# Padding the tiles of split x by 32 bytes, in a Fourier-mixing and mixture-of-experts kernel

## The chip, the core and the metric

The kernel runs on one core of a Trainium2 chip. The metric is device microseconds of one execution; less is better. Before the change the median of 3 timed runs is 762.34 us (760.38 to 762.79).

## What is computed

A layer norm of x (2048 tokens, 512 features) goes through a two-dimensional Fourier transform of which the real part is kept, and x is added. A second layer norm goes through a router that picks one of 8 experts for each token, and that expert's two matrices; the result is added again. In the reference:

```python
a = jnp.einsum("bsd,ed->bse", x, dft_hid_re)
b = jnp.einsum("bsd,ed->bse", x, dft_hid_im)
y = jnp.einsum("ts,bse->bte", dft_seq_re, a) - jnp.einsum("ts,bse->bte", dft_seq_im, b)
...
h = x + _A_ref(_layernorm(x, axis=-1), A_dft_seq_re, A_dft_seq_im, A_dft_hid_re, A_dft_hid_im)
h2 = h + _B_ref(_layernorm(h, axis=-1), B_w_gate, B_w1, B_w2)
```

With one expert per token the softmax over the picked logit is 1, so an expert's output is silu(x w1) w2 for its own tokens.

## The kernel before

Float32 accuracy is reached by splitting each operand into a high part in float32r and the rest, also float32r. `split` (L92) makes both, ScalarE the high part and VectorE the rest, and `mm3` (L129) turns one product into three matmuls: rest of the stationary operand by high part of the moving one (L131), high by rest (L132), high by high (L133). In the trace these three lines carry nearly all of TensorE's work, in every stage; the tiles' names tell the stage.

**The sequence stage**, from about 8 to 447 us of the span. x is normalised and split once, by `start` (L227) and `slot` (L197), into 16 tiles `xh0` to `xh15` and 16 tiles `xl0` to `xl15` of 128 partitions by 512 columns (2,048 bytes per partition), which stay in the pool `keep` (L165, L166). The sequence matrices come in blocks of 128 by 1024 into `raw`, and are split into `whi` and `wlo` (four buffers of each, 4,096 bytes per partition, pool `ring`). There are 8 chunks c of 256 output rows, and 8 blocks g to a chunk. For each block the loop of L482 to L486 goes over the four column groups k of 128, and inside over the two halves u of the block; tile s = 2g + u of x is the stationary operand (128 columns of it), half u of `whi` or `wlo` the moving one with 512 columns, and the four accumulators `p` take turns by k. So three matmuls use tile 2g, then three use tile 2g + 1, then the next k. That makes 8 x 8 x 8 x 3 = 1,536 matmuls of 512 columns. Behind a chunk the four accumulators are split into `ph` and `pl`, and `second` (L399) makes the transform over the features for two tiles of tokens, 24 matmuls each with `ph` and `pl` as stationary operands and `dh` and `dl` as moving ones (L408); it stands between blocks of the next chunk. `finish` (L297) does the residual, the norm and the router's logits.

**Routing.** `place` (L387) makes one-hot tiles of the tokens' ranks. It allocates them under the names `xh0` to `xh15` again, in the places of x tiles that are no longer read. L515 reads 14 of them as moving operands.

**The expert stage**, from about 464 us. Eight experts by 11 blocks of weights, again split into `whi` and `wlo`. `first` (L630) has the weights as stationary operand and the tokens `th`, `tl` as moving ones (256 to 304 columns); `then` (L645) does the second matrix, with the hidden activations `hh`, `hl`. Where the capacity is 256, `then` has `hh` and `hl` as stationary operands and the second half of `whi` and `wlo` as moving ones, 512 columns (L656). The tiles of this stage lie in the pool `moe`, which begins where `keep` began.

PE, VectorE, ScalarE and SP run in the order in which the kernel is written (a manual schedule); no planner and no table moves anything.

**Where the tiles lie.** In the built program the addresses are in bytes within a partition. The four `whi` buffers begin at 52,320, 56,416, 60,512 and 64,608, the four `wlo` at 68,704 to 80,992 in the same steps. `xh0` begins at 85,088, and the 32 tiles of split x follow each other in steps of 2,048. So every tile of split x and every half of `whi` and `wlo` has the same address modulo 2,048, which is 1,120, and modulo 512 it is 96; the 128 columns of a stationary operand begin at a multiple of 512 bytes in the tile. `dh`, `dl`, `ph` and `pl` have 96 modulo 512 too. In the expert stage the three `hh` buffers begin at 107,392, 108,608 and 109,824, the three `hl` at 111,040, 112,256 and 113,472: 288, 480, 160, 352, 32 and 224 bytes, modulo 512, from the halves of `whi` and `wlo`.

Of the kernel before, what the change touches and what calls it, by code (L numbers as in the profile page):

```python
# [9 lines left out]
F32R = mybir.dt.float32r  # L10
# [9 lines left out]
P = 128  # L20
S, D, F, E = 2048, 512, 1376, 8
EPS = 1e-5
NS = S // P
# [12 lines left out]

HOT = (5, 3, 2, 2, 0)
FAR = 2 * S

AHEAD = 7  # L40

# [2 lines left out]
def fnet_moe(ctx: ExitStack, tc: tile.TileContext, x, wseq, dhid, wgate, wcol, wexp, out):  # L44
# [23 lines left out]
    tok = const.tile([P, NS], F32, name="tok")  # L68
    nc.gpsimd.iota(tok, pattern=[[P, NS]], base=-FAR, channel_multiplier=1, allow_small_or_imprecise_dtypes=True)

# [87 lines left out]
    with ExitStack() as pa:  # L158
        keep = pa.enter_context(tc.tile_pool(name="keep", bufs=1))
# [2 lines left out]
        py = pa.enter_context(tc.tile_pool(name="py", bufs=1, space=PSUM))  # L162
        pr = pa.enter_context(tc.tile_pool(name="pr", bufs=1, space=PSUM))

        xh = [keep.tile([P, D], F32R, name=f"xh{s}") for s in range(NS)]  # L165
        xl = [keep.tile([P, D], F32R, name=f"xl{s}") for s in range(NS)]  # L166
        xts = {}

        def load_x(s):
# [215 lines left out]
        places = {}  # L385

        def place(t):  # L387

            q = places[t] = keep.tile([P, D], F32R, name=f"xh{t}")
            for c in ((slice(EARLY, NQ * P), slice(0, EARLY)) if t == NS - 1 else (slice(0, NQ * P),)):  # L390
                nc.vector.tensor_scalar(q[:, c], lanes[:, c], rank[:, t:t + 1], None, op0=ALU.is_equal)

# [6 lines left out]
        def second(t, ph, pl, xt, late=False, between=None):  # L399
            ps = pp.tile([P, D], F32, name="p") if between is not None else py.tile([P, D], F32, name="y")  # L400
            j = t % (TC // P)
            n = 0
            for k in range(KD):
                if k == KD - 1 and between is not None:
                    next(between)
                for im in range(2):
                    col = slice(im * TC + j * P, im * TC + (j + 1) * P)
                    mm3(ps, (ph[k][:, col], pl[k][:, col]), (dh[:, k, im, :], dl[:, k, im, :]), n == 0, n == 2 * KD - 1)  # L408
                    n += 1
            return finish(t, ps, xt, late, t >= NS - 4)  # L410
# [25 lines left out]
        for c in range(NC):  # L436
            ps = [pp.tile([P, 2 * TC], F32, name="p") for _ in range(KD)]
            for g in range(NS // 2):
# [25 lines left out]
                if c == NC - 1:  # L464
                    if g == 1:
                        cards(0, NS - 4)
                        ranks(0, NS - 4, group)
                    for t in range(max(0, 2 * g - 4), 2 * g - 2):
                        place(t)
                advance()  # L470
                if c == NC - 1 and g == NS // 2 - 1:
                    cards(NS - 4, NS - 2)
                    ranks(NS - 4, NS - 2, group)
                    for t in (NS - 4, NS - 3):
                        place(t)
                    nc.vector.tensor_copy(early, seen[:, NL, 0:1])
                    nc.vector.memset(seen[:, NL, 0:1], float(EARLY // P))
# [4 lines left out]
                for k, u in turns:  # L482
                    s = 2 * g + u
# [24 lines left out]
        f = second(NS - 2, ph, pl, last[0], True)  # L508
# [15 lines left out]
        nc.scalar.copy(whole, tb[:, :NQ * 2 * E])  # L524
        nc.gpsimd.tensor_scalar(src0, table[:, :, 0, 0], float(FAR), float(NL * P - 1), op0=ALU.add, op1=ALU.min)

# [3 lines left out]
        def fetch0(to, of, i):  # L530
            n, src, of = (P, src0[:, i:i + 1], of[:NL * P, :]) if i < EARLY // P else (LATE, src1, of)
            nc.gpsimd.indirect_dma_start(
                out=to[:n, i, :], out_offset=None, in_=of, in_offset=bass.IndirectOffsetOnAxis(ap=src[:n, :], axis=0))
# [8 lines left out]
        rk = before_them(NL, NL + 1)  # L542
        ranks(NL, NL + 1, rk)
        place(NL)
        next(g)
        warm = work.tile([P, 1], F32, name="warm")
# [9 lines left out]
        for _ in range(HOT[1]):  # L556
# [6 lines left out]
        nc.vector.tensor_scalar(  # L563
            src1, tb[:, late * 2 * E:late * 2 * E + 1], float(FAR), float(S - 1), op0=ALU.add, op1=ALU.min)
        fetch0(xg0, frows, late)
# [15 lines left out]
    with ExitStack() as pb:  # L581
# [9 lines left out]
        def home(tids):  # L591
            ids = work.tile([P, NQ], I32, name="ids", bufs=3)
            nc.vector.tensor_scalar(ids, tids, float(FAR), None, op0=ALU.add)
            return ids

        def whence(tids):

            src = work.tile([P, NQ], I32, name="src", bufs=3)
            nc.vector.tensor_scalar(src, tids, float(FAR), float(S - 1), op0=ALU.add, op1=ALU.min)
            return src, home(tids)  # L600
# [198 lines left out]
        for n in range(len(steps) + LAG):  # L799
# [26 lines left out]
            if n >= LAG:  # L826
# [12 lines left out]
                if j == 0 and done:  # L839
                    q, yT = done.pop()  # L840
# [3 lines left out]
        q, yT = done.pop()  # L844
# [6 lines left out]
        with tc.For_i(0, blocks, 1):  # L851
# [11 lines left out]
            spot = work.tile([P, NS], F32, name="spot")  # L863
            nc.vector.tensor_scalar(spot, whom, best, float(FAR), op0=ALU.not_equal, op1=ALU.mult)
            nc.vector.tensor_add(spot, spot, rank)
# [4 lines left out]
            for i, (lo, n) in enumerate(both):  # L870
                ps = pt.tile([P, D], F32, name="tp")
                for t in range(NS):
                    q = work.tile([P, P], F32R, name="q")
# [76 lines left out]
```

## Time and profile before

| | before |
|---|---|
| median of 3 timed runs | 762.34 us |
| profiled execution | 754.38 us |
| its span | 752.5 us |
| PE busy | 734.9 us (98%) |
| PE weight loads busy | 636.2 us |
| VectorE busy | 469.1 us |
| ScalarE busy | 260.8 us |
| POOL busy | 185.6 us |
| L131, L132, L133 with `xl`, `xh` | 512 matmuls each, mean 392, 390, 390 ns |
| chunks of data moved | 114.4 MB, mean 152 GB/s |

The profiled execution took 754.38 us, 752.5 of them between the first and the last instruction. Matmuls are pipelined: one is in the array for some 390 ns, while the next starts long before that, so the sum of the means is far more than the busy time, and the distance between starts is what a matmul costs. The granted clock is 1.00 where PE runs at 2.4 GHz, and 0.5 at 1.2 GHz.

### The profile page before, as it was taken

To read this page: it belongs to the slowest core of one execution; us is meant where nothing else is said; L and a number is where in the kernel's file an instruction comes from. 1 tells how busy PE (TensorE), PEld (TensorE's weight loads), DVE (VectorE), ACT (ScalarE), POOL (GpSimd) and SP (SyncE) were. 2 spreads that over 40 slices of the span, in tenths; PEclk is the share of its full clock that TensorE was granted. 3 is DMA by queue.
4 is the path that set the end of the run, shared out by engine and by line. 5 is a ranking of instruction groups with operands and counts; after the bars stand their busy time and mean duration, and the time that the engine had idled before them with its cause. 6 is when DMAs were issued, how large, how long until landed. Compare 5 with 4: busy or idle time off the path is not lost. (4 is left out here: it accounts for less than half of the span.)

```text
span 752.5 us, 10584 instructions
## 1 busy us (share of the span) xinstructions
PE 734.9 (98%) x3998; PEld 636.2 (85%) x3999; DVE 469.1 (62%) x1042; ACT 260.8 (35%) x391; POOL 185.6 (25%) x194
## 2 busy tenths in 40 slices
PE   8999999999999999999999999999999999999993
PEld 5888888888888888888888877999999999999992
DVE  8975754745745736636644566667677787777771
ACT  6872121131121121121121123444545455555550
POOL 3210000000000000000000003648484746647311
PEclk9999999999999999999999998999999999999997
DMA  8646324233323232332322423755666666667610
GB/s 293 238 166 249 118 85 138 90 110 109 125 99 112 99 125 84 122 103 85 126 98 84 141 84 95 241 209 180 219 203 200 213 224 226 230 225 236 210 57 29
DMA packets 34647, 114.40 MB, mean 152 GB/s; under 512 B 4751, under 2 KB 4751, under 8 KB 34464
## 3 DMA queue, kind: packets, MB, share of 16 engines
q0 software_dynamic: 17600, 60.70, 23.7%
q1 hardware_dynamic: 16992, 52.98, 20.2%
q8 instruction: 33, 0.54, 0.3%
q14 instruction: 22, 0.18, 0.1%
HBM read 101.07 MB, written 12.78 MB: 151 GB/s over the span
## 5 line engine op out<-in xcount | busy, mean ns | idle before, releaser
L131 PE MATMUL p<-whi,xl 128*128 128x512 f32 x512 | 200.7, 392 | 0.9 <-DVE xl L265 0.8
L132 PE MATMUL p<-wlo,xh 128*128 128x512 f32 x512 | 199.9, 390 | 0.0
L133 PE MATMUL p<-whi,xh 128*128 128x512 f32 x512 | 199.8, 390 | 0.0
L94 DVE TENSOR_TENSOR wlo<-far,whi 128x1024 fp32r<-128x1024 f32 x77 | 94.3, 1224 | 54.2 <-ACT whi L93 54.1
L131 PEld LDWEIGHTS p<-whi,xl 128*128 128x128 f32 x512 | 96.6, 189 | 21.9 <-DVE xl L265 1.8
L133 PEld LDWEIGHTS p<-whi,xh 128*128 128x128 f32 x512 | 96.6, 189 | 20.3
L132 PEld LDWEIGHTS p<-wlo,xh 128*128 128x128 f32 x512 | 96.6, 189 | 19.9
L93 ACT CAST whi<-far 128x1024 fp32r<-128x1024 f32 x77 | 80.7, 1048 | 75.6 <-PE yp L133 75.6
L111 POOL DMA_INDIRECT far<-in_wexp,wi x77 | 83.5, 1085 | 91.9 <-DVE hh L641 47.8
L131 PE MATMUL hp<-th,wlo 128*128 128x256 f32 (+4 forms) x352 | 101.8, 289 | 0.6 <-ACT ex L698 0.6
L93 ACT CAST whi<-raw 128x1024 fp32r<-128x1024 f32 x66 | 68.4, 1049 | 94.5 <-PE p L133 43.8
L133 PE MATMUL hp<-th,whi 128*128 128x256 f32 (+4 forms) x352 | 100.6, 286 | 0.0
L132 PE MATMUL hp<-tl,whi 128*128 128x256 f32 (+4 forms) x352 | 100.6, 286 | 0.0
L94 DVE TENSOR_TENSOR wlo<-raw,whi 128x1024 fp32r<-128x1024 f32 x66 | 80.0, 1223 | 29.1 <-ACT whi L93 29.1
L319 POOL DMA_DIRECT2D hrows<-row x14 | 7.8, 555 | 328.8 <-DVE row L303 328.8
L131 PEld LDWEIGHTS hp<-th,wlo 128*128 128x128 f32 x352 | 66.3, 188 | 2.5 <-ACT ex L698 0.6
L342 DVE SCALAR_TENSOR_TENSOR xn<-row,wg 128x512 f32<-128x512 f32 x96 | 66.3, 691 | 2.5
L132 PEld LDWEIGHTS hp<-tl,whi 128*128 128x128 f32 x352 | 66.3, 188 | 1.6
L133 PEld LDWEIGHTS hp<-th,whi 128*128 128x128 f32 x352 | 66.2, 188 | 0.0
L137 ACT ACTIVATE std<-mv,eps 128x1 f32<-128x1 f32 (+1 forms) x25 | 7.4, 295 | 167.8 <-DVE mv L307 163.8
L303 DVE TENSOR_TENSOR row<-y,xt 128x512 f32<-128x512 f32 x15 | 10.4, 692 | 84.3 <-PE y L133 84.3
L131 PE MATMUL yp<-hh,wlo 128*128 128x304 f32 (+3 forms) x176 | 52.8, 300 | 0.0
(197 smaller groups left out, 1111.8 us busy)
## 6 DMA issues: line engine op xcount, KB each, us to landing
raw<-in_wseq SPq DMA_DIRECT2D x63, 512.0 KB, 3.4
xt<-in_x SPq DMA_DIRECT2D x32, 256.0 KB, 4.0
raw<-in_wexp SPq DMA_DIRECT2D x11, 512.0 KB, 3.5
hrows<-row POOLq DMA_DIRECT2D x14, 256.0 KB, 2.3
frows<-row POOLq DMA_DIRECT2D x14, 256.0 KB, 2.4
row<-in_dhid SPq DMA_DIRECT2D x4, 512.0 KB, 5.0
wg<-in_wgate SPq DMA_DIRECT2D x1, 2048.0 KB, 12.2
far<-in_wexp,wi POOLq DMA_INDIRECT x77, 5.0
```

The lines of the kernel that those rows point to most:

```text
L93: nc.scalar.copy(hi, src)
L94: (eng or nc.vector).tensor_sub(lo, src, hi.bitcast(F32))
L111: nc.gpsimd.indirect_dma_start(out=raws[b], out_offset=None, in_=wflat, in_offset=bass.IndirectOffsetOnAxis(ap=windex[turn][:, j:j + 1], a ...
L131: nc.tensor.matmul(ps, sl, mh, start=first, stop=False)
L132: nc.tensor.matmul(ps, sh, ml, start=False, stop=False)
L133: nc.tensor.matmul(ps, sh, mh, start=False, stop=last)
L137: nc.scalar.activation(s, var, AF.Sqrt, bias=eps)
L303: nc.vector.tensor_add(h, ps, xt)
L319: q.dma_start(hrows[t * P:(t + 1) * P, :], h)
L342: nc.vector.scalar_tensor_tensor(scr, xf, 1.0, wg[:, e * D:(e + 1) * D], op0=ALU.mult, op1=ALU.mult, accum_out=lg[:, e:e + 1])
```

## The change

Each of the 32 tiles of split x is allocated with 8 more float32r columns (32 bytes per partition) behind its 512, and only the first 512 are used. The tiles that `place` allocates under the same names get the same shape. Nothing else is changed.

```diff
+PAD = 8
...
-        xh = [keep.tile([P, D], F32R, name=f"xh{s}") for s in range(NS)]
-        xl = [keep.tile([P, D], F32R, name=f"xl{s}") for s in range(NS)]
+        xh = [keep.tile([P, D + PAD], F32R, name=f"xh{s}")[:, :D] for s in range(NS)]
+        xl = [keep.tile([P, D + PAD], F32R, name=f"xl{s}")[:, :D] for s in range(NS)]
...
-            q = places[t] = keep.tile([P, D], F32R, name=f"xh{t}")
+            q = places[t] = keep.tile([P, D + PAD], F32R, name=f"xh{t}")[:, :D]
```

In the built program `xh0` stays at 85,088 and the tiles follow in steps of 2,080: tile s of `xh` has 96 + 32 s modulo 512, and so has tile s of `xl` (`xl0` is at 118,368). `dh` and all that lies behind it in `keep` and in the pool `work` moves by 1,024 bytes; the pools `const`, `ring` and `moe` stay where they are. Each engine's instructions stand in the same order as before. On PE, VectorE, ScalarE and POOL five instructions name other semaphores in their waits, four of them at first uses of the pool `moe` (the first write of `th` by ScalarE, of `tl` by VectorE, the first L131 of the expert stage, and the first `far` gather), one in the last loop, which has no work in this profile.

## Rows read from the trace of the kernel before

**Rows 1.** The page: busy time by engine, and the granted clock.

```profile
PE 734.9 (98%) x3998; PEld 636.2 (85%) x3999; DVE 469.1 (62%) x1042; ACT 260.8 (35%) x391; POOL 185.6 (25%) x194
...
PEclk9999999999999999999999998999999999999997
```

**Rows 2.** Busy time by stretch; the first row names the columns.

```profile
core 0: us, PE busy (x) PEld busy (x) DVE busy (x) ACT busy (x) POOL busy (x), PEclk, DMA share, GB/s
20.00:60.00 40.00, 39.96 (x177) 32.73 (x176) 33.46 (x75) 30.52 (x47) 7.88 (x6) 1.00 0.62 225
100.00:150.00 50.00, 50.00 (x223) 41.40 (x222) 26.14 (x59) 9.89 (x13) 2.16 (x4) 1.00 0.29 100
600.00:650.00 50.00, 50.00 (x357) 46.64 (x357) 37.66 (x71) 26.58 (x43) 29.01 (x26) 1.00 0.66 219
```

**Rows 3.** Timeline of PE, sequence stage: start, length, engine, line, operation.

```profile
99.66 0.39 PE L133 MATMUL p<-whi,xh 128*128 128x512 f32 x1
99.89 0.39 PE L131 MATMUL p<-whi,xl 128*128 128x512 f32 x1
...
111.90 0.39 PE L133 MATMUL p<-whi,xh 128*128 128x512 f32 x1
```

**Rows 4.** Timeline of PE, the stage's first matmuls.

```profile
8.94 0.63 PE L133 MATMUL p<-whi,xh 128*128 128x512 f32 x1
9.36 0.63 PE L131 MATMUL p<-whi,xl 128*128 128x512 f32 x1
```

**Rows 5.** Timeline of PE, sequence stage, behind two other matmuls.

```profile
385.54 0.21 PE L359 MATMUL rk<-seen,ones 128*128 128x96 bf16 x1
385.57 0.47 PE L131 MATMUL p<-whi,xl 128*128 128x512 f32 x1
385.88 0.39 PE L132 MATMUL p<-wlo,xh 128*128 128x512 f32 x1
386.11 0.40 PE L133 MATMUL p<-whi,xh 128*128 128x512 f32 x1
386.35 0.40 PE L131 MATMUL p<-whi,xl 128*128 128x512 f32 x1
...
387.96 0.39 PE L132 MATMUL p<-wlo,xh 128*128 128x512 f32 x1
...
389.10 0.39 PE L131 MATMUL p<-whi,xl 128*128 128x512 f32 x1
```

**Rows 6.** Timeline of PE, expert stage, two runs of 512 columns.

```profile
654.89 0.40 PE L131 MATMUL yp<-whi,hl 128*128 128x512 f32 x1
655.12 0.40 PE L132 MATMUL yp<-wlo,hh 128*128 128x512 f32 x1
...
656.28 0.28 PE L131 MATMUL hp<-th,wlo 128*128 128x256 f32 x1
...
641.03 0.40 PE L132 MATMUL yp<-wlo,hh 128*128 128x512 f32 x1
...
642.20 0.28 PE L131 MATMUL hp<-th,wlo 128*128 128x256 f32 x1
```

**Rows 7.** Groups of PE by line and shape: busy us, mean ns of one.

```profile
L132 PE MATMUL p<-wlo,xh 128*128 128x512 f32 x512 | 199.9, 390 | 0.0
...
L132 PE MATMUL yp<-wlo,hh 128*128 128x512 f32 x88 | 34.8, 396 | 0.0
```

**Rows 8.** Timeline of PE, expert stage, 304 columns.

```profile
476.05 0.30 PE L131 MATMUL yp<-hh,wlo 128*128 128x304 f32 x1
...
477.30 0.31 PE L131 MATMUL hp<-th,wlo 128*128 128x304 f32 x1
```

**Rows 9.** Timeline of all engines, routing and the first write of the expert stage.

```profile
448.93 2.58 PE L515 MATMUL p<-xh,mine 128*16 128x384 f32 x14
...
460.06 0.59 ACT L93 CAST th<-p 128x512 fp32r<-128x512 f32 x1 [4.98 <-PE p L573]
```

## Prediction

> **What bounds the kernel now.** First the page: TensorE is busy for 734.9 of 752.5 us [rows 1]. Then the stretches: from 100 to 150 us the DMA engines are busy 29% of the time, VectorE 26 of 50 us, ScalarE 10, and PE the whole 50, at a granted clock of 1.00, which is 2.4 GHz [rows 2]. Nothing else can end last there, so the time of the sequence stage is a count of matmuls times the distance from one matmul's start to the next. I call that distance the gap. The "0.39" behind a start is the length of one matmul through the pipe, and matmuls overlap; only starts add up.
>
> So the view that matters is the timeline of PE, read by its starts. In [rows 3] there are 54 gaps between 99.66 and 111.90 us: 12.24 us / 54 = 226.7 ns. 512 columns at 2.4 GHz are 213.3 ns, so 13.3 ns of each gap are something else. At the start, before the clock has risen, the same matmuls are 0.43 us apart [rows 4]; 512 columns at 1.2 GHz are 426.7 ns, so there nothing is left over.
>
> The 226.7 is strikingly even. 1,473 of the 1,536 gaps of the sequence stage behind an L131 to L133 matmul with an x tile as its stationary operand are 226 or 227 ns; the others are the first ones, the two or three behind a pause, and what follows a pause. That last is the key row: after the two small matmuls of L359 the gaps are not 226.7 but swing between 224 and 236, 9 of them from 385.88 to 387.96, 2.08 us, a mean of 231.1 ns; then they are 226.7 again and stay there [rows 5]. Four pauses and the rise of the clock are followed by 6 to 10 such gaps, three pauses by none. So 226.7 is a state that this stream falls into and keeps, not a price of each matmul.
>
> What is special in this stream? All its addresses agree: every x tile and every half of the weights' buffers lies at the same offset modulo 512 bytes (the kernel section has them). The expert stage has the same 512-column matmuls with the same moving operands (the second halves of whi and wlo), but with hh and hl as stationary operands, which lie 32, 160, 224, 288, 352 or 480 bytes (modulo 512) from them. There it never settles: from 654.89 to 656.28 six gaps take 1.39 us, 231.7 each, and from 641.03 to 642.20 five take 1.17, 234 each [rows 6]. Of 41 such runs of six, the second to fifth gap (164 in all) have a mean of 232.7. Their records are longer too, 396 ns against 390 for L132 [rows 7].
>
> Is that the stage (more DMA, more VectorE) or the offsets? For the offsets: between 20 and 60 us, with DMA as busy as in the expert stage (0.62 and 0.66) and ScalarE and VectorE busier, the sequence stage has 177 matmuls in 40 us, the same pace as 223 in 50 [rows 2]; and in the expert stage the order of gaps repeats with the set of buffers (229, 235, 231, 236, 234, 231 comes back seven times, to 1 ns, with the same hh and hl). And the narrower matmuls, whose tiles also lie at changing offsets, pay the same: nine gaps of 304 columns take 1.25 us, 138.9 each [rows 8]. If the settled stream is scaled down, 226.7 x 304/512 = 134.6; they are 4.3 over it, as the 512s of that stage are 6 over 226.7.
>
> **The change, part by part.** It moves no instruction: each engine has the same rows in the same order as before. What differs:
>
> 1. The stationary operands' addresses. Tile s of xh and of xl moves by 32 s bytes (modulo 512), so against the weights' halves the 16 tiles take all 16 multiples of 32, tile 0 alone keeps 0. A step of the inner loop takes tiles 2g and 2g+1 in turn, three matmuls each, so the offset changes with every third matmul. Six of the 16 offsets (tiles 1, 5, 7, 9, 11, 15) are just those of hh and hl above. Settling took 6 to 10 gaps where all offsets agree, so three matmuls would not be enough for it even if each offset had its own settled state. I therefore take the gaps as unsettled. Low price: the mean behind the pause, 231.1 - 226.7 = 4.4 ns; 1,473 x 4.4 = 6.5 us. High price: the run of 234, 7.3 ns; 1,473 x 7.3 = 10.8 us. Nearest is the expert stage's mean, 6.0 ns, since buffers and shape are the same, but it shows only offsets that are odd multiples of 32; for the even half I keep the lower one. (4.4 + 6.0) / 2 = 5.2 ns, x 1,473 = **7.7 us**. Nothing covers it: PE is without a pause there [rows 2].
>
> 2. The second transform (L408) keeps its offsets: dh, dl, ph and pl move by 1,024 bytes together, which is 0 modulo 512. But its 16 groups of 24 matmuls now start from an unsettled stream and need some 6 gaps to settle, at 4.4 ns: 16 x 6 x 4.4 = **0.4 us**.
>
> 3. place() writes into the padded tiles. L515 reads 14 of them as moving operands, 2.58 us in all [rows 9]; even 5% of that is 0.1 us. Counted as nothing.
>
> 4. Waits. The first tiles of the expert stage lie where x tiles lay, and with other borders a few first writers name fewer or other semaphores, ScalarE's first th cast among them. In the trace that cast is released by PE's transposes of L573 [rows 9], which stay, so no gain: 0, at most the 0.1 us by which one more name could cost.
>
> 5. 1,024 bytes more per partition, all of it behind the x tiles. No buffer is lost and no transfer starts at another time, except that a slower PE frees the weights' buffers later, and DMA has 71% idle there [rows 2].
>
> Sum: 7.7 + 0.4 = 8.1 us. On the profiled execution (754.38 us, of which 752.5 are the span) that gives 762.5. The median of the timed runs is 762.34, 8.0 above the profiled one; the difference is not explained by any row and I add the sum to the median: 770.4 us, 1.1% slower.
>
> **A rule against any effect.** The row: with 512 columns and the same moving buffers the gap is 226.7 at one offset [rows 3] and about 232 at others [rows 6]. The Trainium skill, "TensorE: Matmul & The Clock Gate", Part 2, step 1 (LDWEIGHTS), says that TensorE has two independent read ports into SBUF and that loading the next weights takes nothing from the running matmul. By that rule the stationary address could not matter, the difference in [rows 6] would be the stage's, and the sum would be 0 instead of 8.1; that is the first rival.
>
> **Rivals.**
> Nothing happens: the gap of 226.7 belongs to 512 columns repeated without a pause, whatever the offsets; the expert stage's runs of six are merely too short to settle (a settling took up to 10 gaps). For it: the three pauses after which no settling was needed. Against it: the 304-column rounds run for hundreds of matmuls without settling, and the sequence of gaps follows the buffers. Time: 762.3, plus or minus 1.
>
> Faster, the other side: equal offsets make the weight load and the stream meet in the same place of SBUF, and that is the 13.3 ns over 213.3. With offsets spread, all of it would go: 1,473 x 13.3 = 19.6 us, 742.7; with half of the tiles freed, 752.5. It decides from the point at which unequal offsets have gaps under 226.7. For it: at the lower clock nothing is over [rows 4]. Against it: the 6 of 16 offsets that the trace shows have longer gaps, not shorter, and no run of six has a mean under 226.7. The same page, section "Back-to-back issue gap", gives N / 2.4 + 2.5 ns, 215.8 for 512 columns; by it the gain would be an estimated 16 us. The traces have no stretch at that pace.
>
> Half of it: only odd multiples of 32 disturb, and the even tiles settle at once: 1,473 / 2 x 6.0 = 4.4 us, 766.7. Against it: odd and even alternate every three matmuls.
>
> **How the numbers follow.** Everything unsettled: 0.62, 768.9 to 773.2. Half of it: 0.18, about 766.7. Nothing: 0.12. Faster: 0.08. A measurement of this kernel can tell about 0.3%, 2.3 us, from no change. Slower by more than that: 0.62 + 0.18 = 0.80; within: 0.12; faster: 0.08. The range reaches from the lower edge of "nothing" to a little over the high price (762.3 + 10.8 + 0.4 = 773.5): 761.5 to 774; the faster case and edges are left out, under 2 in 10.
>
> **What would show it.** Right: in the sequence stage the starts are uneven, 224 to 237 ns apart, mean about 232, some 217 matmuls' worth of time in 50 us where there was 223; L131 to L133 with x tiles have means near 395 ns instead of 390; y of L408 settles again; the sequence stage ends 8 us later and the expert stage is as long as before. Wrong: gaps of 226 or 227 throughout (nothing), or under 226 (faster). A change in the expert stage or between 446 and 464 us would mean that I missed a wait.

## The result

The changed kernel takes 769.93 us (median of 4 runs, 768.31 to 770.37) against 761.91 us before: a ratio of 1.0104, 95% interval 1.0081 to 1.0126. It is 8.0 us slower.

The page of the changed kernel, busy time by engine and the three costliest groups, which answer to [rows 1] and [rows 7] (line numbers are two higher; the last numbers of a group are its busy us and the mean ns of one):

```profile
span 768.5 us, 10568 instructions
...
PE 745.9 (97%) x3999; PEld 637.8 (83%) x3999; DVE 469.3 (61%) x1042; ACT 259.9 (34%) x391; POOL 181.6 (24%) x194
...
L133 PE MATMUL p<-whi,xl 128*128 128x512 f32 x512 | 203.1, 397 | 1.9 <-DVE xl L267 1.9
L134 PE MATMUL p<-wlo,xh 128*128 128x512 f32 x512 | 202.6, 396 | 0.0
L135 PE MATMUL p<-whi,xh 128*128 128x512 f32 x512 | 202.5, 395 | 0.0
```

VectorE's and ScalarE's busy times are as before. What got longer are the matmuls with x tiles: 397, 396 and 395 ns where they had 392, 390 and 390. L134's 396 is just the number that L132 had in the expert stage before [rows 7].

Busy time by stretch of the changed kernel, which answers to [rows 2]:

```profile
core 0: us, PE busy (x) PEld busy (x) DVE busy (x) ACT busy (x) POOL busy (x), PEclk, DMA share, GB/s
20.00:60.00 40.00, 40.00 (x174) 32.39 (x173) 32.88 (x76) 31.40 (x49) 7.76 (x6) 1.00 0.60 216
100.00:150.00 50.00, 50.00 (x218) 40.64 (x217) 24.95 (x58) 9.96 (x14) 2.16 (x4) 1.00 0.27 95
```

PE is busy for the whole of both, as before (to 0.04 us), at the same granted clock of 1.00 (2.4 GHz), but gets through 218 matmuls in 50 us instead of 223. A PE that is 100% busy is thus no proof that it runs at its best pace. The timeline of PE, which answers to [rows 3]:

```profile
200.17 0.39 PE L133 MATMUL p<-whi,xl 128*128 128x512 f32 x1
200.40 0.39 PE L134 MATMUL p<-wlo,xh 128*128 128x512 f32 x1
...
202.95 0.40 PE L133 MATMUL p<-whi,xl 128*128 128x512 f32 x1
```

From 200.17 to 202.95 there are 12 gaps in 2.78 us, 231.7 ns each, where 54 gaps had a mean of 226.7. Over the whole stage, the 1,536 gaps behind a matmul with an x tile sum to 350.9 us before and 358.7 after: 7.8 us more. Without the first few at the lower clock and those of 300 ns and more their mean goes from 226.8 to 232.2 ns, and of the 1,473 that were 226 or 227 only 54 are left.

### The profile page after: what moved, and what is told of

Same layout as the page of the kernel before. It is cut to its first block, busy times and chain, and to the rows that moved or that the text cites. A ratio compares the mean times of both kernels' runs of the same rounds, so it can differ in the third digit from the quotient of the medians.

```text
span 768.5 us, 10568 instructions
## 1 busy us (share of the span) xinstructions
PE 745.9 (97%) x3999; PEld 637.8 (83%) x3999; DVE 469.3 (61%) x1042; ACT 259.9 (34%) x391; POOL 181.6 (24%) x194
## 5 line engine op out<-in xcount | busy, mean ns | idle before, releaser
L133 PE MATMUL p<-whi,xl 128*128 128x512 f32 x512 | 203.1, 397 | 1.9 <-DVE xl L267 1.9
L134 PE MATMUL p<-wlo,xh 128*128 128x512 f32 x512 | 202.6, 396 | 0.0
L135 PE MATMUL p<-whi,xh 128*128 128x512 f32 x512 | 202.5, 395 | 0.0
L133 PEld LDWEIGHTS p<-whi,xl 128*128 128x128 f32 x512 | 96.6, 189 | 25.7 <-DVE xl L267 3.1
L134 PEld LDWEIGHTS p<-wlo,xh 128*128 128x128 f32 x512 | 96.7, 189 | 22.4
L133 PE MATMUL hp<-th,wlo 128*128 128x256 f32 (+4 forms) x352 | 102.8, 292 | 3.9 <-DVE wlo L96 2.5
L113 POOL DMA_INDIRECT far<-in_wexp,wi x77 | 81.7, 1061 | 98.4 <-DVE hh L643 51.1
L134 PE MATMUL hp<-tl,whi 128*128 128x256 f32 (+4 forms) x352 | 101.3, 288 | 0.0
L133 PEld LDWEIGHTS hp<-th,wlo 128*128 128x128 f32 x352 | 66.9, 190 | 6.7 <-DVE wlo L96 3.4
L134 PEld LDWEIGHTS hp<-tl,whi 128*128 128x128 f32 x352 | 66.9, 190 | 2.0 <-issue 0.3
L640 ACT ACTIVATE sl<-hp 128x256 f32<-128x256 f32 (+4 forms) x88 | 34.7, 394 | 62.6 <-PE hp L135 47.2
```

Source lines behind the costliest of these rows:

```text
L113: nc.gpsimd.indirect_dma_start(out=raws[b], out_offset=None, in_=wflat, in_offset=bass.IndirectOffsetOnAxis(ap=windex[turn][:, j:j + 1], a ...
L133: nc.tensor.matmul(ps, sl, mh, start=first, stop=False)
L134: nc.tensor.matmul(ps, sh, ml, start=False, stop=False)
L135: nc.tensor.matmul(ps, sh, mh, start=False, stop=last)
L640: nc.scalar.activation(sl, ps, AF.Silu)
```

## The experiments

Every group of runs had its own runs of the kernel before on its own chip; chips differ by more than the change does (before: 761.9, 755.7, 764.7 and 755.7 us), so times are compared inside a group only. A gap is the distance between the starts of two matmuls, as in the prediction. "Mean gap" is that of the sequence stage's matmuls with x tiles, without the start and pauses (gaps of 300 ns and more).

**e1, the room alone.** The tiles stay as they were, and 1,024 bytes are put behind them.

```diff
         xl = [keep.tile([P, D], F32R, name=f"xl{s}") for s in range(NS)]
+        gap = keep.tile([P, 256], F32, name="gap")
```

> The x tiles stay in steps of 2,048 bytes, and one unused tile of 1,024 bytes behind xl15 moves everything behind them as the change does. All offsets keep 0 modulo 512. Both theories (the changing offset, the offset itself) expect the time of before, 761.9 us within 2, with gaps of 226 or 227 ns in the sequence stage. Rival, that the room taken or the moved second transform costs something: slower, up to 770.

756.35 us against 755.74, ratio 1.0009 (0.9996 to 1.0023); mean gap 226.8. The room, and the move of all that lies behind it, cost nothing that the interval shows. The 8 us are the x tiles' own places.

**e2 and e3, one constant offset.** 32 (e2) or 64 bytes (e3) ahead of `xh0`; all x tiles move together.

```diff
+        gap = keep.tile([P, 8], F32, name="gap")
         xh = [keep.tile([P, D], F32R, name=f"xh{s}") for s in range(NS)]
```

> One unused tile of 32 bytes ahead of xh0: all x tiles have the one offset 32 from the weights' halves, and it never changes. Theory A (my step 1: what keeps the stream from settling is that the offset changes with every third matmul): it settles, gaps of 226.7 ns, 761.9 us as before. Theory B (the offset itself sets the pace, and 32 has none of 226.7): gaps as in the changed kernel's first block, where offset 32 stood for twelve matmuls in a row at a mean of 233.6 ns; 6.9 ns x 1,473 = 10 us, 772 us.

> As the run before, with 64 bytes. Theory A: 226.7 ns, 761.9 us. Theory B: the changed kernel's twelve matmuls in a row at offset 64 were 233 or 234 ns apart, 233.3 on the mean; 6.6 ns x 1,473 = 9.8 us, 771.7 us. If only odd multiples of 32 bytes did harm: 761.9 us.

e2: 765.31 us against 755.74, ratio 1.0125 (1.0101 to 1.0149). e3: 766.39 us, ratio 1.014 (1.0119 to 1.0161). Theory A, which is the reason that I gave in step 1, has fallen: an offset that never changes costs at least as much as one that changes all the time. The timeline of PE in e2, then in e3:

```profile
200.01 0.40 PE L131 MATMUL p<-whi,xl 128*128 128x512 f32 x1
200.25 0.40 PE L132 MATMUL p<-wlo,xh 128*128 128x512 f32 x1
200.48 0.40 PE L133 MATMUL p<-whi,xh 128*128 128x512 f32 x1
...
205.85 0.40 PE L132 MATMUL p<-wlo,xh 128*128 128x512 f32 x1
```

```profile
200.28 0.39 PE L131 MATMUL p<-whi,xl 128*128 128x512 f32 x1
200.51 0.39 PE L132 MATMUL p<-wlo,xh 128*128 128x512 f32 x1
...
205.88 0.39 PE L131 MATMUL p<-whi,xl 128*128 128x512 f32 x1
```

In e2 25 gaps take 5.84 us, 233.6 each; in e3 24 take 5.60, 233.3. These streams are settled too, only at another pace: in this stretch of e3 every gap is 233 or 234 ns (nearly four in five over the whole stage), in e2 the gaps alternate between 235 and 231 or 232. The mean over the stage is 233.3 in both. The rival "only odd multiples of 32 disturb" has fallen with e3.

**e4, an offset that changes by 256 bytes.** Even tiles first, 256 bytes, then the odd ones.

```diff
+        xh, xl = {}, {}
+        for u in range(2):
+            if u:
+                gap = keep.tile([P, 64], F32, name="gap")
+            for s in range(u, NS, 2):
+                xh[s] = keep.tile([P, D], F32R, name=f"xh{s}")
+                xl[s] = keep.tile([P, D], F32R, name=f"xl{s}")
```

> Even x tiles keep offset 0, odd ones lie 256 bytes further, so the offset changes with every third matmul, by 256. Theory A: unsettled, mean about 232 ns, 769.7 us. Theory B with a period of 256 bytes (in the changed kernel the mean gap at offset s is that at s + 256 to within 2 ns): gaps of 226.7 ns, 761.9 us.

754.95 us against 755.74, ratio 0.9995 (0.9985 to 1.0005); mean gap 226.8, 1,467 of them 226 or 227. The offset changes with every third matmul, as in the changed kernel, and nothing is lost:

```profile
199.74 0.39 PE L131 MATMUL p<-whi,xl 128*128 128x512 f32 x1
199.97 0.39 PE L132 MATMUL p<-wlo,xh 128*128 128x512 f32 x1
...
202.01 0.39 PE L132 MATMUL p<-wlo,xh 128*128 128x512 f32 x1
```

Ten gaps in 2.27 us are 227.0 ns. So an offset of 256 is as good as 0. That all offsets repeat after 256 bytes, to within 2.3 ns, is what the changed kernel says when its gaps are sorted by the offset of the x tile, with the next matmul's tile at the same offset (worked out from the starts of its matmuls and the addresses of the built program):

| offset modulo 256 | mean gap at s, ns | at s + 256, ns |
|---|---|---|
| 0 | 228.6 | 228.5 |
| 32 | 233.5 | 232.5 |
| 64 | 233.3 | 233.6 |
| 96 | 232.2 | 231.7 |
| 128 | 233.8 | 231.5 |
| 160 | 234.3 | 234.5 |
| 192 | 229.1 | 229.2 |
| 224 | 234.6 | 234.9 |

Settled streams were run at 0, 32 and 64 bytes, and at 256 in turn with 0; the other rows are means of a stream whose offset changes.

**e5, an offset that changes by 32 bytes.** As e4 with 32 bytes for 256. One execution was profiled and none timed beside it, so only the gaps count.

```diff
-                gap = keep.tile([P, 64], F32, name="gap")
+                gap = keep.tile([P, 8], F32, name="gap")
```

> Even x tiles keep offset 0, odd ones lie 32 bytes further. By the runs so far (the offset modulo 256 sets the pace): the odd half at the 233.3 ns of the constant 32, the even half, were it settled, at 226.7: a mean of 230, 1,473 x 3.3 = 4.9 us slower than before. If switching between offsets costs besides, since the even tiles have only three matmuls to settle in: even ones at about 231, a mean of 232 and 8 us.

The mean gap is 231.3 ns, between the two expectations (230 and 232). With current and next tile at offset 32 it is 233.0; with both at 0 it is 228.3 instead of 226.7. From a tile at 0 to one at 32 it is 230.0, from 32 to 0 235.2. So half of the tiles at a bad offset cost more than half: the good ones, three at a time, do not get back to 226.7. That is the part of my reason that stands.

**e7, xl tiles alone.** 64 bytes between `xh15` and `xl0`. Here too one execution was profiled and none timed beside it.

```diff
         xh = [keep.tile([P, D], F32R, name=f"xh{s}") for s in range(NS)]
+        gap = keep.tile([P, 16], F32, name="gap")
         xl = [keep.tile([P, D], F32R, name=f"xl{s}") for s in range(NS)]
```

> An unused tile of 64 bytes between xh15 and xl0: xh tiles keep offset 0, xl tiles have 64. If the load of the next matmul's weights meets the running stream, only the gap of L133, during which an xl tile is loaded, gets longer: 233.3 there and 226.7 twice, a mean of 228.9, 3.3 us slower than before. If a matmul's own stationary tile counts: the gap of L131 instead. If every change of offset disturbs all that follows: about 231 on all three lines, 6.6 us.

The mean gap is 231.0 ns. None of the three simple patterns came out: the gap of L131 is 235 to 236, those of L132 and L133 are 228.6 and 229.3, and a settled round of three takes 693.3 where e4 has 680. The timeline of PE and of its weight loads (PEld) shows two rounds of three, 1.38 us by the rows from 200.04 to 201.42:

```profile
200.04 0.40 PE L131 MATMUL p<-whi,xl 128*128 128x512 f32 x1
200.04 0.19 PEld L132 LDWEIGHTS p<-wlo,xh 128*128 128x128 f32 x1
200.27 0.39 PE L132 MATMUL p<-wlo,xh 128*128 128x512 f32 x1
200.28 0.19 PEld L133 LDWEIGHTS p<-whi,xh 128*128 128x128 f32 x1
200.50 0.39 PE L133 MATMUL p<-whi,xh 128*128 128x512 f32 x1
200.50 0.19 PEld L131 LDWEIGHTS p<-whi,xl 128*128 128x128 f32 x1
200.73 0.40 PE L131 MATMUL p<-whi,xl 128*128 128x512 f32 x1
...
201.42 0.40 PE L131 MATMUL p<-whi,xl 128*128 128x512 f32 x1
```

The longest gap is that of the matmul whose own stationary tile is off, at 64. By the rows the load that runs beside it is that of an `xh` tile at offset 0 (200.04); the load of the `xl` tile runs beside L133 (200.50), whose gap is 229.3. In e5 the order is the same: 235.2 with the tile in use off and the loaded one at 0, 230.0 the other way round. So the load of a tile at another offset beside the running stream doesn't account for the longest gap. But the two other gaps of e7 are longer than 226.7 as well, and what in the chip lengthens them all stays open.

**e9, all addresses together.** 416 bytes at the end of `wg` take the weights' buffers, the x tiles and the second transform's tiles from 96 to 0 modulo 512.

```diff
     wg = const.tile([P, E * D], F32, name="wg")
+    gap = const.tile([P, 104], F32, name="gap")
```

> An unused tile of 416 bytes at the end of the wg tile moves the weights' buffers, the x tiles, dh, dl, ph and pl together, from 96 to 0 modulo 512; the offsets between them stay 0. If only the offset between stationary and moving tile counts: gaps of 226.7 ns and the time of before. If the address itself counts: another pace in the sequence stage, the next lower multiple of 6.67 ns being 220, 9.8 us faster, the next higher 233.3, 9.8 us slower.

755.51 us against 755.72, ratio 0.9997 (0.9984 to 1.001); mean gap 226.8. So it is the offset between the tiles that counts and not where they lie, as far as these two places show.

**e6, the expert stage set to offset 0.** The tokens' and activations' tiles get 320 columns, 1,280 bytes or 5 x 256, and places that are 0 modulo 256 from the weights' buffers; x tiles as before.

```diff
+ROOM = 320
...
+        hid = pb.enter_context(tc.tile_pool(name="hid", bufs=3))
...
-            hh = work.tile([P, CAP], F32R, name="hh", bufs=3)[:, :n]
-            hl = work.tile([P, CAP], F32R, name="hl", bufs=3)[:, :n]
+            hh = hid.tile([P, ROOM], F32R, name="hh")[:, :n]
+            hl = hid.tile([P, ROOM], F32R, name="hl")[:, :n]
```

> The other way round: x tiles as before, and in the expert stage th, tl, hh and hl get 320 columns of room instead of 304, in places that are all 0 modulo 256 from the weights' buffers. If the offset modulo 256 sets the pace there too: 512 columns go from 232.7 to 226.7 ns (some 248 gaps, 1.5 us), 256 columns from 118.4 to 113.3 (some 511 gaps, 2.6 us), if six or twelve in a row are enough to settle; the widths between them settle only on a multiple of the 6.67 ns that 226.7, 233.3 and 113.3 have in common, and gain less. 2 to 5 us faster than before. If the expert stage's pace is the stage's own (its DMA, its VectorE): no change.

767.44 us against 764.73, ratio 1.003 (1.001 to 1.005): not faster, a little slower. The widths moved, though. Summed over the expert stage's gaps without waits, the time over 17/16 of the columns at 2.4 GHz (what 226.7 is for 512) fell from some 8.8 us to 8.0. 304 columns went from 4.9 to 3.4 ns over it, 264 from 5.1 to 3.7, 512 from 6.1 to 5.0, but 256 rose from 5.2 to 5.9. The timeline of PE shows why (line numbers are one higher):

```profile
645.58 0.28 PE L132 MATMUL hp<-th,wlo 128*128 128x256 f32 x1
645.69 0.28 PE L133 MATMUL hp<-tl,whi 128*128 128x256 f32 x1
645.81 0.28 PE L134 MATMUL hp<-th,whi 128*128 128x256 f32 x1
...
646.89 0.28 PE L134 MATMUL hp<-th,whi 128*128 128x256 f32 x1
647.01 0.38 PE L620 MATMUL tp<-ident,xg 128*128 128x128 f32 x2
```

From 645.69 to 647.01 eleven gaps take 1.32 us, 120.0 each; here they repeat a pattern, and most of the other rounds of 256 columns settle on 120 ns gap by gap (313 gaps in all), not on 113.3. And 512 columns, six in a row, seem to have no time to settle: 28 of the 41 runs have 234, 236, 228, 232, 231 as their first five gaps, to within 1 ns, and 236, 228, 233, 230 is how the sequence stage of the kernel before ends its settling, from 387.04 to 387.96 us in the stretch of [rows 5]. The small gain was lost to waits: 16 gaps over 330 ns in the expert stage behind its first matmuls, against 8 in e7 and in e8, which ran on the same chip. Its list of waits has, for PE:

```profile
PE hp L132 <- DVE wlo L95: 3.2, 5, 1.5
...
PE yp L133 <- issue: 2.4, 4, 0.9
PE hp L132 <- issue: 2.0, 3, 1.1
```

Why there are more of them (other tiles share the places of the first gathers) was not tried.

**e8, e10 and e11, the profiles again.** The profiled executions of before and after differ by 16.0 us, twice the timed difference. Nearly all of the other half is the expert stage, which takes 283.0 us from its first matmul to its last, against 275.6: PE waits in it, which the profile of before does not show, and behind the waits it runs at the lower clock. The waits of PE in the changed kernel from 460 us on (engine, line, waited for: us in total, times, longest):

```profile
PE hp L133 <- DVE wlo L96: 2.5, 3, 1.7
PE hp L133 <- issue: 1.4, 2, 1.2
PE yp L135 <- issue: 0.6, 1, 0.6
```

The longest of them in the timeline of PE, then the busy time by stretch around it in the changed kernel and in the kernel before (columns as in [rows 2]):

```profile
530.97 0.29 PE L134 MATMUL yp<-hl,whi 128*128 128x280 f32 x1
531.10 0.29 PE L135 MATMUL yp<-hh,whi 128*128 128x280 f32 x1
533.07 0.60 PE L133 MATMUL hp<-th,wlo 128*128 128x280 f32 x1 [1.67 <-DVE wlo L96]
533.47 0.43 PE L134 MATMUL hp<-tl,whi 128*128 128x280 f32 x1
533.70 0.43 PE L135 MATMUL hp<-th,whi 128*128 128x280 f32 x1
```

```profile
520.00:550.00 30.00, 26.27 (x186) 24.93 (x186) 15.89 (x27) 10.77 (x17) 14.19 (x13) 0.94 0.52 174
```

```profile
511.00:541.00 30.00, 30.00 (x231) 29.18 (x230) 19.86 (x37) 13.38 (x22) 18.09 (x15) 1.00 0.61 208
```

The granted clock is 0.50, 1.2 GHz, from 532.6 to 536.0 us, and the same 280 columns then start 0.23 us apart where they had 0.13; from 471.5 to 531 us it is 1.00.

> The changed kernel once more, to see whether the 4.5 us in which TensorE waited between 525 and 534 us of its profile belong to it. If they do (another wait at the first uses of the expert stage's tiles): the same waits at the same place. If they are one execution's: no such waits, an expert stage as long as that of before within 1 us, and a sequence stage 8 us longer.

> The kernel before once more, profiled on the chip of the next run. If the waits of TensorE in the expert stage (4 to 5 us behind about 520 us in the profile of the changed kernel and in three of the experiments) are the chip's and not the change's: the same waits here, if this chip is one of the slower ones (before at 760 or more), and none if it is a faster one (about 756). Sequence stage as before, 226.7 ns.

> The changed kernel on the same chip as the two runs before. Sequence stage at a mean of 232.2 ns, ending 7.8 to 8.4 us later than that of the run before; expert stage as long as there, within 1 us; time 1.0104 of before's within the interval of the first comparison.

e8 is the changed kernel on the chip of e5 to e7, and it has these waits (3.1 us in 5, the longest 1.6); so have e5 and e7 at the same place, 521 to 530 us of their spans. e10 and e11 are the two kernels on one of the faster chips, and neither has them; their lists name for the expert stage only the wait for its first tokens, in e10 and in e11:

```profile
PE hp L131 <- ACT th L93: 0.3, 1, 0.3
```

```profile
PE hp L133 <- ACT th L95: 0.3, 1, 0.3
```

There the spans are 753.7 and 762.0, 8.3 us apart, the mean gaps 226.8 and 232.2, and the timed ratio is 1.0106 (1.0077 to 1.0136). Two details were expected otherwise. The sequence stage ends 8.8 us later, of which 0.7 is a later start, and the expert stage is 1.3 us shorter in e11 than in e10. The granted clock goes with the latter: in e10 it is 0.50 from 463.2 to 466.6 us, in the first matmuls of that stage, in e11 from 463.0 to 473.2, ahead of it, and there the routing is 1.6 us longer. That the waits go with the chip and not with the change is thus shown for the changed kernel, which has them on the chip of e8 and not on that of e11. For the kernel before it is likely, since the ratio is 1.0104 in the comparison whose profile has them and 1.0106 in the one without; a profile of before on a chip that has them was not taken.

## Why the prediction was right, point by point

**The sum.** Step 1 had 5.2 ns for each of 1,473 gaps, 7.7 us; measured are 232.2 - 226.8 = 5.4 ns and 7.8 us. Step 2 had 0.4 us for the second transform; its 384 gaps went from a mean of 226.7 to 227.4, 0.3 us. Steps 3 to 5 had nothing. For step 5, e1 shows nothing for the room and for what moves with it; steps 3 and 4 have no run of their own, but the first two steps leave nothing for them in the 8.0 us. 8.1 us were forecast, 8.0 measured. The signs came too: 218 matmuls in 50 us where 217 were forecast, and means of 395 to 397 ns for 395. The one that didn't, an expert stage as long as before, failed in the profiled execution by 7.4 us of waits and lower clock, not in the timed ratio (e11).

**What the forecast rested on held in part.** That another offset alone lengthens the gaps of 512 columns is shown: in e2 and e3 it is the sequence stage that has the long gaps, with the DMA and VectorE of that stage. The size came from the runs of six of the expert stage [rows 6], 232.7 there and 232.2 in the changed kernel. But e6 took the offset out of those runs and only 1.1 of their 6.1 ns over 226.7 went with it. So their 6 ns were not the price of the offset alone; what else is in them, settling by the look of e6, was not taken apart.

**The reason in step 1 was wrong in its main part.** I put the loss down to the offset changing with every third matmul, so that the stream never settles. e4 changes it as often and loses nothing; e2 and e3 never change it and lose 9.6 and 10.7 us. The offset itself sets the pace, modulo 256. The changing offset comes on top: with it, tiles at offset 0 have 228.3 to 228.6 instead of 226.7 (e5 and the table). That the size came out right is in part luck. Of the two prices that I averaged, 4.4 came from a stream at offset 0 that settles behind a pause [rows 5], and 6.0 from runs of six, most of whose excess e6 left in place. I gave 6.0 to the odd multiples of 32 and 4.4 to the even ones; in the table the odd ones have a mean of 233.5, 6.8 over 226.7, and the even ones 231.0, 4.3 over it. The even ones are cheaper for a reason that I didn't have: 0 and 192 are cheap, while 64 costs as much as an odd one.

**The rule against any effect.** With the same instructions and the same moving tiles, 512 columns take 226.7 ns at offset 0 or 256 (e4) and 233.3 at 32 or 64 (e2, e3). So the stationary operand's address does play a part, 6.6 ns in each matmul, and the rival "nothing happens" falls. The Trainium skill, "TensorE: Matmul & The Clock Gate", Part 2, step 1 (LDWEIGHTS), says that the moving operand and LDWEIGHTS have independent read ports and that loading the next weights takes no SBUF read bandwidth from the running matmul. What the prediction drew from it, that the address could not matter, disagrees with the traces; the statement itself they don't refute, since in e5 and e7 it is not the load of the next tile that goes with the longest gap.

**The rival "faster".** It decided from the point at which other offsets have gaps under 226.7. None of the 16 has a mean under it: the best of them, 0, 192 and their partners, are at 228.5 to 229.2 in the changed kernel. For 512 columns equal offsets were the best case, not the conflict. The 13.3 ns over 213.3 at the full clock are there at every offset, and no run here shows a stream without them.

## What to carry to other kernels

Where PE is busy all the time, read the distance between the starts of its matmuls and compare it over the stages: the same shape at two paces is time to be had or lost, and busy shares don't show it. For float32r matmuls of 512 columns in a long stream, keep stationary and moving tiles at the same offset modulo 256 bytes, in particular when a pool is padded or a small tile is put between; the price of not doing so was 5.4 to 6.6 ns in 226.7. It is no rule for every stream: in e6 it gave 1.1 ns in runs of six, and 256 columns became 0.7 ns slower, so read the gaps again afterwards. And an even, settled pace can hold for the wrong reason as well: test a reason by a version that keeps the suspected cause and takes the other away (e4 against e2), not by the size of the effect alone.

## What the runs showed that I had not expected

The streams that settle fall into patterns whose length is, to within the 1 ns of the records, a multiple of 6.67 ns, which is 16 columns at 2.4 GHz: 226.7 is 34 of them, 233.3 in e3 is 35, the pair 235 + 232 of e2 is 70, the three gaps of e7 are 104 (693.3), and 256 columns in e6 are 18 (120.0). In the first four blocks the loop has the halves outside and the column groups inside (L479, L480 before), which the kernel section leaves out, so there twelve matmuls in a row use one tile and have one offset. In the changed kernel offset 192 repeats 225, 230, 231, which is 103, and offset 160 repeats 231, 238, 231, which is 105. So in these streams an offset costs nothing or whole steps, shared among the matmuls of its pattern. What has that period in the chip, no run here tells.
